# Opening and end of an attention reordered: key rows of 256 bytes, the second half of the keys turned in step 1, first weights converted seven steps sooner

## The chip and the metric

The kernel runs on one core of a Trainium2 chip. The metric is the device time of one execution in microseconds, lower is better; the times shown are medians over repeated executions. The core has five engines with a queue of instructions each: TensorE (PE in the profile, PEld for its weight loads) for matmuls and transposes, VectorE (DVE), ScalarE (ACT), GpSimd (POOL), and SyncE (SP), which here issues nearly all DMAs. Each engine works through its own queue in the order in which the program was written, so an instruction that waits holds everything behind it on that engine. The profile is one execution recorded by the hardware profiler; its times count from the start of the span.

## The reference

Attention with a bias that depends on positions, and behind it two small feed-forward blocks. B = 2, H = 8 heads, S = 576 tokens, D = 64; all inputs are float32, and the two weight groups of the feed-forward blocks come as float64.

```python
scores = scale * q @ k.T                                   # (B, H, S, S)
x = log1p(|i - j|) / log1p(max(i, 1))                      # (S, S), one number per pair
bias = relu(x * w1 + b1) @ w2                              # hidden 32 -> 8 heads
attn = softmax(scores + bias)                              # sum + 1e-9 below
x = concat_heads(attn @ v)                                 # (1152, 512)
y = ((x @ w_a) * (x @ w_b)) @ w_out                        # 512 -> 1536 -> 512
h = y @ w_in                                               # 512 -> 1024
solu = h * softmax(h);  ln = (solu - mean) / sqrt(var + 1e-6) * g_ln
out = ln @ w_out2                                          # 1024 -> 512
```

## The kernel before

Products in float32 precision are made from pairs of rounded parts: a value is split into a high part (float32r) and a low part, the difference, and TensorE multiplies the parts.

**The order.** Nothing is scheduled by a planner: the program writes each engine's order out by hand. After a preamble come nine turns T = 0 to 8 of an opening, then a loop over steps n = 0 to 76. Step n works on several stages of the pipeline at once. There are nine units (a block of 128 query rows of one batch; the last unit, number 8, has 64 rows of each batch), each of eight steps, one per head: 72 steps, and the loop runs on for five drain steps. A string, ORDER, gives the order of the parts in a step: b is the biased scores and their minimum of step n-1 on VectorE (L401), h the reciprocal of the sums and the scaling of step n-2 on POOL (shares, L413 to L415), p the exponential of step n-1 on ScalarE (L408), t the transposes of step n-3 (L423, L432) with copies out, s the scores of step n on TensorE (L388), v the values of a pair of heads (L452), o and u the bias, k and l the two halves of queries and keys turned in the step before, i and j the output of a finished unit, and x whatever was put down for the step by `later`.

**Bias.** A table (tabs) of x * w1 for all distances is made by matmuls with one row (`table`); the part for small row numbers comes first, the low part later. For each of 36 groups of 16 rows (T), `bias_hidden` makes four tiles h by Relu (L351 on VectorE, L353 on ScalarE, chosen by HIDDEN), `bias_sums` multiplies them by w2bd, a block matrix made by POOL from w2 (L213), and `bias_out` scales the sums by rp (made by `scales`, L221) into st on ScalarE (L371) and sends st by DMA into the bias tile of 128 rows. Groups 0 to 7 are made in the opening; a unit's first biased scores need all eight. SECOND_T gives the steps for groups 8 to 15.

**Keys and queries.** `fetch` loads a chunk of 128 tokens of four heads (a group g is four heads; ks[b, g] is four chunks and a short one of batch b). `twice` makes the high and the low part of a chunk (L268, L269; for queries a copy on POOL, L271), `turn` transposes it on TensorE (L281), and `keep_high` copies it into kst, the transposed keys (ScalarE, L298), or into qhi (L305); `keep_low` makes qlo on VectorE (L318). Group ks[0, 0] and the first queries (first_in) are turned in the opening; ks[0, 1] with the second queries (second) behind it; ks[1, 0] and ks[1, 1] in the steps that KEYS gives, with `twice` one step before. One DMA brings a whole group except its short chunk: each partition takes four neighbouring rows of a head, 1024 bytes, so that chunk c holds every fourth token, and its copy into kst writes with a stride of four:

```python
cols = slice(c, NC * P, NC) if c < NC else slice(NC * P, S)
nc.scalar.copy(kst[:, u, g * HG:(g + 1) * HG, cols], ps)
```

**First weights.** The words of the first four pieces of w_a and w_b (float64, two chunks c of 128 columns) are loaded and turned into float32 during the last unit by `first_one`, a generator of six stages: the load; Abs on ScalarE (L97) and a clamp on VectorE (L98); one word operation on VectorE (L103); two more (L105, L106); the high part on ScalarE (L566); the low part on VectorE (L568). FIRST gives the steps of the stages, counted from step 64. EARLY gives the steps, counted from 64 too, in which three blocks `gated(c, tg)` of 24 matmuls are put between the last parts of the attention; `product` follows each one step later. The space for these words is that of the h and st tiles, after step 56. All other pieces (the third chunk first) are loaded after the last values of the attention, into space which these free, and converted by `convert` while TensorE runs the other gated blocks. Tiles of scores, bias sums, tables and gated blocks share two PSUM buffers in turn (ps_s); those of transposes share three (ps_t).

Of the kernel before, what the change touches and what calls it, by code (L numbers as in the profile page):

```python
# [17 lines left out]
P = 128  # L18
# [7 lines left out]
ORDER = ("kbhvioljptsxu", "kbihlospjtvxu")  # L26
TURN = 55

KEYS = (4, 5, 5, 6, 7, 7, 8, 9, 11, 11)
SECOND_T = (1, 3, 6, 8, 10, 12, 13, 14)  # L30
LAST_T = (48, 50, 52, 54)

HIDDEN = (("vava", "vvva", "vvva", "vvvv", "vvva", "vvvv", "vvva", "vava"), ("vvvv", "avvv"))

FIRST = ((0, 1, 2, 3, 6, 7), (0, 3, 4, 5, 6, 7), (1, 6, 7, 8, 10, 11), (4, 7, 8, 8, 11, 11))
# [5 lines left out]
EARLY = {(0, 0): 8, (0, 1): 10, (1, 0): 11}  # L41
# [12 lines left out]
def tile_kernel(ctx, tc, q, k, v, w1, b1, w2, w_a, w_b, w_out, w_in2, w_out2, g_ln, psi, rpsi, out):  # L54
# [101 lines left out]
    with ExitStack() as actx:  # L156
# [27 lines left out]
        nc.scalar.dma_start(psi_i, psi[:, UW:].rearrange("(o c) t -> o c t", o=1))  # L184
        nc.scalar.dma_start(b1r, b1.rearrange("(o m) -> o m", o=1))
        nc.scalar.activation(warm, ident[:, 0:1], AF.Exp)
# [4 lines left out]
        nc.scalar.dma_start(rp_in, rpsi)  # L191

# [22 lines left out]
        def scales():  # L215

            ps = ps_t.tile([P, 4, NG // 16], F32, tag="t", name="ps_rp")
            for c in range(4):
                for qd in range(4):
                    nc.tensor.matmul(ps[32 * qd:32 * qd + 32, c], order4[:, c].rearrange("p g h -> p (g h)"), rp_in[:, qd::4], start=True, stop=True)  # L220
            nc.vector.tensor_copy(rp.rearrange("p (c k) -> p c k", c=4), ps)  # L221

        kst = ac.tile([P, B, H, S], F32R, name="kst")
# [8 lines left out]
        def fetch(w):  # L232
# [3 lines left out]
            if src == "k" and c < NC:  # L236

                if c == 0:
                    nc.sync.dma_start(raws[at, g], k[at, heads, 0:NC * P, :].rearrange("h (p r) d -> p h (r d)", r=NC))
                fetched[w] = raws[at, g][:, :, c * D:(c + 1) * D]  # L240
                return
# [17 lines left out]
        def twice(w, engine=nc.gpsimd):  # L259

            nat = fetched[w]
            if w[0] == "k":
                if w[3] < NC:
                    x, nat = nat, room(w)
                    fetched[w] = nat
                else:
                    x = nat[:, :, 1, :]
                nc.vector.tensor_copy(nat[:, :, 0, :].bitcast(F32R), x)  # L268
                engine.tensor_tensor(out=nat[:, :, 1, :], in0=x, in1=nat[:, :, 0, :], op=ALU.subtract)  # L269
                return  # L270
            nc.gpsimd.tensor_scalar(nat[:, :, 1, :], nat[:, :, 0, :], 1.0, 1.0, op0=ALU.mult, op1=ALU.mult)  # L271
# [20 lines left out]
        def keep_high(w):  # L292
# [3 lines left out]
            if src == "k":  # L296
                cols = slice(c, NC * P, NC) if c < NC else slice(NC * P, S)
# [184 lines left out]
        for b in range(B):  # L482
            for g in range(2):
                i = b * 2 + g
                raws[b, g] = arena[0][:, i * nr:(i + 1) * nr].rearrange("p (h x) -> p h x", h=HG)
# [4 lines left out]
        for w in first_in + second:  # L490
            fetch(w)
        nc.sync.dma_start(psi_l, psi[3:4, low + 3 - 12:half + 3])
        N0 = P // 16
        for j in range(2):
            nc.gpsimd.memset(vtl[(1 - j) * TL:(2 - j) * TL, :, :, j, :], 0.0)
        made = [[w] for w in first_in] + [second[0:3], second[3:5], second[5:]]
        for T in range(N0 + 1):
            if T < N0:
                bias_hidden(T)
            for w in made[T]:  # L500
                twice(w, nc.vector if w in first_in else nc.gpsimd)
            if T == 1:
                scales()
            if T > 0:
# [4 lines left out]
                if T <= len(first_in):  # L509
                    keep(first_in[T - 1])  # L510
            if T == 6:
                for dst, ps in table(low, half - low, psi_l, low - 12):
                    nc.scalar.copy(dst, ps)
# [4 lines left out]
        for w in second:  # L518
            turn(w)
            keep(w)  # L520
# [17 lines left out]
        for T in range(N0, S // 16):  # L538
# [8 lines left out]
            out_at.setdefault(n + 1, []).append(T)  # L547
        steps = [(u, h) for u in range(len(units)) for h in range(H)]
# [43 lines left out]
        for n in range(len(steps) + 5):  # L592
            for part in ORDER[n >= TURN]:
# [363 lines left out]
```

## Time and the profile before

| | |
|---|---|
| median of 3 runs | 553.75 us (553.64 to 553.91) |
| the profiled execution | 554.66 us |
| its span, first to last instruction | 552.8 us |
| TensorE busy | 534.8 us, 97% |
| VectorE busy | 421.4 us, 76% |
| ScalarE busy | 291.4 us, 53% |
| GpSimd busy | 173.9 us, 31% |

The attention takes the first 223 us or so, the feed-forward blocks the rest. Shares are means over stages with different limits; "busy" of TensorE counts the modelled length of pipelined matmuls. A row of a timeline gives the start and length in us, engine, line, operation, the tile written and the tiles read, how many such instructions follow one another, and, in brackets, the idle time of the engine before them with what ended it. Listed lengths on one engine can overlap by about 0.1 us. SPq and ACTq are DMA issues from the queues of SyncE and ScalarE.

### The profile page before, as it was taken

The numbers are of one execution on the slowest core, as the hardware profiler recorded it, in microseconds if no ns is written. First come the engines' busy times: TensorE is split into PE (matmuls) and PEld (weight loads), VectorE is DVE, ScalarE is ACT, GpSimd is POOL, SyncE is SP. The second block draws the span as 40 slices with busy tenths as digits, with TensorE's granted clock in tenths as the row PEclk, the third lists the DMA queues.
The fourth block names the chain that finished last, engine by engine and source line by source line (L and its number), as shares of the span: only waits on it lengthen the run. The fifth ranks groups of instructions, "written<-read, shape, count | busy, mean of one in ns | idle before, by whom it ended". The sixth has DMA issues, their size and how long they took to land.

```text
span 552.8 us, 12368 instructions
## 1 busy us (share of the span) xinstructions
PE 534.8 (97%) x4868; PEld 473.1 (86%) x4868; DVE 421.4 (76%) x895; ACT 291.4 (53%) x592; POOL 173.9 (31%) x277
## 2 busy tenths in 40 slices
PE   6978999999999998999999999999999999999997
PEld 2556788888888888999999999999999988888887
DVE  3858899999997687497799898889885566666661
ACT  4878877878787663445555334532443433222221
POOL 3237554545446642122222122233222530000000
PEclk9999999999999998999999999999999999999999
DMA  4494543332347110543445343444310000000001
GB/s 116 121 235 87 118 107 75 77 71 70 83 119 198 34 42 1 160 147 120 151 147 154 116 151 116 127 136 157 114 39 2 0 1 20 20 19 20 19 20 57
DMA packets 47581, 49.32 MB, mean 89 GB/s; under 512 B 23198, under 2 KB 37795, under 8 KB 47524
## 3 DMA queue, kind: packets, MB, share of 16 engines
q1 hardware_dynamic: 47238, 48.52, 31.3%
q8 instruction: 38, 0.62, 0.5%
q14 instruction: 19, 0.16, 0.1%
q10 hardware_dynamic: 286, 0.03, 0.1%
HBM read 34.37 MB, written 2.36 MB: 66 GB/s over the span
## 4 chain that ended last, share of the span: by engine, by line
PE 74%; DVE 10%; issue 3%; ACT 2%; POOL 2%; DMA 0%; DVEq 0%; ACTq 0%; POOLq 0%
PE pm L124 27%; PE po L124 11%; PE py L854 9%; PE ph L794 9%; PE px L452 4%; PE pt L423 4%; PE s L388 4%; PE bps L361 3%; DVE e L401 3%; POOL e L415 2%; DVE h L351 2%; PE pl L835 1%; DVE et L428 1%; PE tp_q L281 1%; ACT kst L298 1%
## 5 line engine op out<-in xcount | busy, mean ns | idle before, releaser
L98 POOL TENSOR_SCALAR f<-f 128x512 f32<-128x512 f32 x48 | 41.3, 862 | 140.2 <-ACT f L97 130.4
L415 POOL TENSOR_SCALAR e<-e,rec 128x576 f32<-128x576 f32 x72 | 60.2, 837 | 70.1 <-DVE rec L414 68.1
L124 PE MATMUL pm<-xhi,abh 128*128 128x384 f32 x240 | 80.2, 334 | 0.0
L124 PE MATMUL pm<-xhi,abl 128*128 128x384 f32 x240 | 80.2, 334 | 0.0
L124 PE MATMUL pm<-xlo,abh 128*128 128x384 f32 x240 | 80.2, 334 | 0.0
L408 ACT ACTIVATE e<-e,nm 128x576 f32<-128x576 f32 x72 | 55.8, 775 | 27.9 <-DVE nm L401 21.3
L351 DVE TENSOR_SCALAR h<-tabs 128x576 f32<-128x576 f32 x122 | 67.0, 590 | 0.0
L401 DVE CUSTOM_DVE_ANT_0 e<-s,bias 128x576 f32<-128x576 f32 x72 | 54.0, 749 | 7.6 <-PE s L388 5.8
L423 PE MATMUL pt<-ident,e 128*128 128x128 f32 x288 | 45.5, 281 | 5.6 <-POOL e L415 4.0
L143 ACT COPY one<-pm 128x384 f32<-128x384 f32 x36 | 17.3, 480 | 61.4 <-PE pm L124 61.4
L124 PE MATMUL po<-gh,oh 128*128 128x384 f32 x144 | 48.5, 337 | 0.6 <-DVE x2s L725 0.6
L124 PE MATMUL po<-gl,oh 128*128 128x384 f32 x144 | 48.4, 336 | 0.0
L124 PE MATMUL po<-gh,ol 128*128 128x384 f32 x144 | 48.4, 336 | 0.0
L361 PE MATMUL bps<-h,w2bd 128*32 128x288 f32 x576 | 47.2, 427 | 1.0 <-DVE nm L401 0.6
L124 PEld LDWEIGHTS pm<-xlo,abh 128*128 128x128 f32 x240 | 45.0, 188 | 0.0
L124 PEld LDWEIGHTS pm<-xhi,abh 128*128 128x128 f32 x240 | 45.0, 188 | 0.0
L124 PEld LDWEIGHTS pm<-xhi,abl 128*128 128x128 f32 x240 | 45.0, 188 | 0.0
L423 PEld LDWEIGHTS pt<-ident,e 128*128 128x128 f32 x288 | 32.2, 140 | 14.2 <-POOL e L415 8.4
L106 DVE SCALAR_TENSOR_TENSOR f<-words,f 128x512 int32<-128x512 int32 x48 | 42.2, 879 | 1.6
L388 PE MATMUL s<-kst,qhi 128*128 128x288 f32 x160 | 40.4, 334 | 0.3 <-ACT st L371 0.2
L452 PE MATMUL px<-et,vsb 128*32 128x128 f32 (+1 forms) x1280 | 40.3, 263 | 0.1
L452 PEld LDWEIGHTS px<-et,vsb 128*32 128x32 f32 x1280 | 34.1, 110 | 7.1 <-issue 1.9
(136 smaller groups left out, 1246.3 us busy)
## 6 DMA issues: line engine op xcount, KB each, us to landing
bias<-st SPq DMA_DIRECT2D x40, 288.0 KB, 3.5
words<-in_moe_w_out_dram SPq DMA_DIRECT2D x20, 512.0 KB, 3.7
words<-in_moe_w_a_dram SPq DMA_DIRECT2D x12, 512.0 KB, 3.4
words<-in_moe_w_b_dram SPq DMA_DIRECT2D x12, 512.0 KB, 3.6
words<-in_moe_w_in_dram SPq DMA_DIRECT2D x8, 512.0 KB, 3.7
nat_q<-in_q_dram SPq DMA_DIRECT2D x16, 128.0 KB, 3.4
arena_hi<-in_k_dram SPq DMA_DIRECT2D x4, 512.0 KB, 4.5
vsb<-in_v_dram SPq DMA_DIRECT2D x16, 128.0 KB, 3.8
```

The lines of the kernel that those rows point to most:

```text
L106: nc.vector.scalar_tensor_tensor(out=b, in0=words[:, :, 0], scalar=29, in1=b, op0=ALU.logical_shift_right, op1=ALU.bitwise_or)
L124: nc.tensor.matmul(ps, w, x, start=(i == 0), stop=(i == n - 1))
L351: nc.vector.tensor_scalar(h, win, sc, 0.0, op0=ALU.add, op1=ALU.max)
L361: nc.tensor.matmul(bps[32 * qd:32 * qd + 32, a, 0:SH], w2bd, h[:, a * SH:(a + 1) * SH], start=True, stop=True)
L388: nc.tensor.matmul(ps[:, a, 0:SH], w, kst[:, b, h, a * SH:(a + 1) * SH], start=(m == 0), stop=(m == len(mm) - 1))
L401: nc.vector.tensor_tensor_reduce(out=halves(e), in0=ps[:, :, 0:SH], in1=halves(bias_t[it][:, h, :]), op0=ALU.add, op1=ALU.min, scale=1.0, ...
L408: nc.scalar.activation(e, e, AF.Exp, bias=nm, scale=-1.0, accum_out=sums[:, h:h + 1])
L415: nc.gpsimd.tensor_scalar(e, e, rec[:, h:h + 1], 1.0, op0=ALU.mult, op1=ALU.mult)
L423: nc.tensor.transpose(pt[:, c, :], e[:, j * TL + c * P:j * TL + (c + 1) * P], ident)
L452: nc.tensor.matmul(px[rows, p, cols], lhsT, rhs, start=(c == 0 and m == 0), stop=(c == NC), skip_group_check=True)
L794: nc.tensor.matmul(ph[u][:, a], x[:, kc, cols], w[:, kc, a * 512:(a + 1) * 512], start=(i == 0), stop=(i == 3 * KD - 1))
L854: nc.tensor.matmul(ps, x[:, c, :], w[:, c, cols], start=(i == 0), stop=(i == 3 * KF - 1))
```

## The change

- The four chunks of a key group come by four DMAs with rows of 256 bytes, and a chunk holds 128 neighbouring tokens, so its copy into kst is dense.
- The DMAs of b1 and psi_i move from ScalarE's queue to SP's; on ScalarE's queue w2 and rp_in come ahead of the load of the exp table. rp is made before the opening's turns and copied by ScalarE.
- In the opening keep_low of the first queries comes one turn later; the vtl memsets move to turn 2; the low table moves from turn 6 to turn 8, copied by VectorE; the second group is fetched in pieces in turns 0 to 4; HIDDEN gives two more Relu of the first eight groups to ScalarE.
- The second group's keys are converted by VectorE alone, just ahead of step 0, and turned and kept in part x of step 1. The sums of group 8 move from step 1 to step 0.
- The keys of batch 1 are converted by POOL alone (before: the cast on VectorE, the subtraction on POOL), and KEYS moves most of them by a step.
- FIRST moves the conversion of the first weights from steps 64 to 75 to steps 57 to 69; EARLY moves two of the three gated blocks one step forward; from step 72 on part x comes ahead of t and v.

```diff
-ORDER = ("kbhvioljptsxu", "kbihlospjtvxu")
-TURN = 55
-KEYS = (4, 5, 5, 6, 7, 7, 8, 9, 11, 11)
-SECOND_T = (1, 3, 6, 8, 10, 12, 13, 14)
+ORDER = ("kbhvioljptsxu", "kbihlospjtvxu", "kbihlospjxtvu")
+TURN, DRAIN = 55, 72
+KEYS = (5, 6, 6, 7, 7, 8, 9, 10, 11, 11)
+SECOND_T = (0, 3, 6, 8, 10, 12, 13, 14)
-HIDDEN = (("vava", "vvva", "vvva", "vvvv", "vvva", "vvvv", "vvva", "vava"), ("vvvv", "avvv"))
-FIRST = ((0, 1, 2, 3, 6, 7), (0, 3, 4, 5, 6, 7), (1, 6, 7, 8, 10, 11), (4, 7, 8, 8, 11, 11))
+HIDDEN = (("vvva", "vvva", "vvva", "vvva", "vvva", "vvva", "vava", "vava"), ("vvvv", "avvv"))
+FIRST = ((-7, -6, -5, -4, 1, 2), (-7, -5, -4, -3, 2, 3), (-6, -3, -2, -1, 3, 4), (-2, 0, 1, 2, 4, 5))
-EARLY = {(0, 0): 8, (0, 1): 10, (1, 0): 11}
+EARLY = {(0, 0): 8, (0, 1): 9, (1, 0): 10}
@@ preamble
-        nc.scalar.dma_start(psi_i, psi[:, UW:].rearrange("(o c) t -> o c t", o=1))
-        nc.scalar.dma_start(b1r, b1.rearrange("(o m) -> o m", o=1))
-        nc.scalar.activation(warm, ident[:, 0:1], AF.Exp)
+        nc.sync.dma_start(b1r, b1.rearrange("(o m) -> o m", o=1))
+        nc.sync.dma_start(psi_i, psi[:, UW:].rearrange("(o c) t -> o c t", o=1))
         nc.scalar.dma_start(w2r, w2.rearrange("(o m) h -> o m h", o=1).to_broadcast([4, HID, H]))
         nc.scalar.dma_start(rp_in, rpsi)
+        nc.scalar.activation(warm, ident[:, 0:1], AF.Exp)
@@ scales
-            nc.vector.tensor_copy(rp.rearrange("p (c k) -> p c k", c=4), ps)
+            nc.scalar.copy(rp.rearrange("p (c k) -> p c k", c=4), ps)
+        scales()
@@ fetch
-                if c == 0:
-                    nc.sync.dma_start(raws[at, g], k[at, heads, 0:NC * P, :].rearrange("h (p r) d -> p h (r d)", r=NC))
-                fetched[w] = raws[at, g][:, :, c * D:(c + 1) * D]
+                fetched[w] = raws[at, g][:, c]
+                nc.sync.dma_start(fetched[w], k[at, heads, c * P:(c + 1) * P, :].rearrange("h p d -> p h d"))
@@ twice
-        def twice(w, engine=nc.gpsimd):
+        def twice(w, engine=nc.gpsimd, rounds=nc.gpsimd):
-                nc.vector.tensor_copy(nat[:, :, 0, :].bitcast(F32R), x)
+                rounds.tensor_scalar(nat[:, :, 0, :].bitcast(F32R), x, 1.0, 1.0, op0=ALU.mult, op1=ALU.mult)
@@ keep_high
-                cols = slice(c, NC * P, NC) if c < NC else slice(NC * P, S)
+                cols = slice(c * P, min(S, (c + 1) * P))
@@ the opening
-        for w in first_in + second:
+        for w in first_in:
             fetch(w)
-        for j in range(2):
-            nc.gpsimd.memset(vtl[(1 - j) * TL:(2 - j) * TL, :, :, j, :], 0.0)
-        made = [[w] for w in first_in] + [second[0:3], second[3:5], second[5:]]
+        made = [[w] for w in first_in] + [second[0:1], [], []]
         for T in range(N0 + 1):
             if T < N0:
                 bias_hidden(T)
             for w in made[T]:
-                twice(w, nc.vector if w in first_in else nc.gpsimd)
-            if T == 1:
-                scales()
+                twice(w, nc.vector if w in first_in else nc.gpsimd, nc.vector)
+            if T > 1 and T - 2 < len(first_in):
+                keep_low(first_in[T - 2])
             if T > 0:
                 bias_sums(T - 1)
                 if T <= len(first_in):
                     turn(first_in[T - 1])
                 bias_out(T - 1)
                 if T <= len(first_in):
-                    keep(first_in[T - 1])
-            if T == 6:
+                    keep_high(first_in[T - 1])
+            if T == 2:
+                for j in range(2):
+                    nc.gpsimd.memset(vtl[(1 - j) * TL:(2 - j) * TL, :, :, j, :], 0.0)
+            if T == N0:
                 for dst, ps in table(low, half - low, psi_l, low - 12):
-                    nc.scalar.copy(dst, ps)
+                    nc.vector.tensor_copy(dst, ps)
+            for w in second[T + (T > 0):T + 2 if T < 5 else T + 1]:
+                fetch(w)
...
-        for w in second:
-            turn(w)
-            keep(w)
+        def turn_second():
+            for w in second:
+                turn(w)
+                keep(w)
+
+        later(1, turn_second)
...
+        for w in second[1:]:
+            twice(w, nc.vector, nc.vector)
         steps = [(u, h) for u in range(len(units)) for h in range(H)]
...
-            for part in ORDER[n >= TURN]:
+            for part in ORDER[(n >= TURN) + (n >= DRAIN)]:
```

## Rows read from the trace of the kernel before

**Rows 1.** Table of stretches: stretch, its length, busy us of each engine, clock.

```profile
core 0: us, PE busy (x) PEld busy (x) DVE busy (x) ACT busy (x) POOL busy (x), PEclk, DMA share, GB/s
32.00:48.00 16.00, 11.75 (x125) 8.06 (x124) 11.46 (x30) 10.93 (x22) 8.82 (x15) 1.00 0.86 196
174.00:186.00 12.00, 11.93 (x185) 10.24 (x187) 8.31 (x25) 9.13 (x23) 9.18 (x20) 1.00 0.52 152
206.40:213.00 6.60, 4.06 (x17) 4.05 (x17) 6.53 (x16) 2.93 (x7) 3.12 (x4) 0.74 0.01 2
```

**Rows 2.** Timeline of the opening, 0 to 26 us.

```profile
2.39 0.59 ACTq L190 DMA_DIRECT2D raw<-in_w_dram  x1
...
6.95 1.85 POOL L213 TENSOR_SCALAR w2bd<-raw 32x8 f32<-32x8 f32 x4 [5.26 <-DMA raw<-in_w_dram]
...
8.85 2.17 PE L361 MATMUL bps<-h,w2bd 128*32 128x288 f32 x16 [0.46 <-POOL w2bd L213]
...
12.74 0.69 DVE L318 SCALAR_TENSOR_TENSOR qlo<-tp_q,qhi 128x512 fp32r<-128x512 f32 x1 [3.43 <-ACT qhi L305]
...
15.04 1.20 PE L361 MATMUL bps<-h,w2bd 128*32 128x288 f32 x16
...
17.01 0.28 DVE L268 CAST arena_lo<-arena_hi 128x256 fp32r<-128x256 f32 x1
...
17.68 1.37 DVE L351 TENSOR_SCALAR h<-tabs 128x576 f32<-128x576 f32 x3
...
22.96 0.96 PE L201 MATMUL table<-psi_l,psi_r 1*32 1x224 f32 x16
```

**Rows 3.** Groups of ScalarE instructions, 0 to 32 us: count, busy us, mean ns.

```profile
L298 ACT CAST kst<-tp_k 128x512 fp32r<-128x512 f32 x8 | 8.5, 1136 | 0.1
L371 ACT ACTIVATE st<-bps,rp 128x576 f32<-128x576 f32 x8 | 5.9, 741 | 4.5 <-PE bps L361 3.7 <-ACT st L371 0.7
L353 ACT ACTIVATE h<-tabs 128x576 f32<-128x576 f32 x8 | 5.8, 768 | 0.8 <-DVE tabs L210 0.8
```

**Rows 4.** Timelines of TensorE, ScalarE and VectorE, 27 to 40 us.

```profile
27.06 0.66 PE L281 MATMUL tp_q<-ident,nat_q 128*128 128x128 f32 x4
...
27.86 0.59 ACT L305 ACTIVATE qhi<-tp_q 128x512 fp32r<-128x512 f32 x1
...
32.00 0.76 DVE L401 CUSTOM_DVE_ANT_0 e<-s,bias 128x576 f32<-128x576 f32 x1 [1.11 <-DMA vsb<-in_v_dram]
...
39.22 0.29 DVE L268 CAST arena_hi<-arena_hi 128x256 fp32r<-128x256 f32 x1 [3.03 <-DMA arena_hi<-in_k_dram]
```

**Rows 5.** DMA issues over the span: count, KB each, median us to landing.

```profile
bias<-st SPq DMA_DIRECT2D x40, 288.0 KB, 3.5
...
words<-in_moe_w_a_dram SPq DMA_DIRECT2D x12, 512.0 KB, 3.4
...
nat_q<-in_q_dram SPq DMA_DIRECT2D x16, 128.0 KB, 3.4
```

**Rows 6.** Timelines of VectorE and TensorE, 205 to 209 us.

```profile
206.00 0.43 DVE L98 TENSOR_SCALAR single<-single 128x512 f32<-128x512 f32 x1 [1.94 <-ACT single L97]
...
208.95 0.69 PE L423 MATMUL pt<-ident,e 128*128 128x128 f32 x4 [2.54 <-POOL e L415]
```

**Rows 7.** Groups of POOL instructions, whole span: count, busy us, mean ns.

```profile
L271 POOL TENSOR_SCALAR nat_q<-nat_q 128x256 f32<-128x256 f32 x18 | 8.4, 471 | 0.1
...
L269 POOL TENSOR_TENSOR arena_hi<-arena_hi 128x256 f32<-128x256 f32 x4 | 3.3, 834 | 2.8 <-DVE arena_hi L268 2.8
```

**Rows 8.** Timelines of VectorE and TensorE, 237 to 241 us.

```profile
237.89 0.68 DVE L111 TENSOR_TENSOR abl<-f,abh 128x512 fp32r<-128x512 f32 x1
...
240.12 0.33 PE L124 MATMUL pm<-xhi,abh 128*128 128x384 f32 x1
```

**Rows 9.** Busy time of the conversions' tile (single) alone, 190 to 221 us: VectorE, ScalarE.

```profile
190.00:221.00 31.00, 12.59 (x20) 4.91 (x8) 0.94 0.06 19
```

**Rows 10.** Timelines of SP's queue and ScalarE, 175 to 178 us.

```profile
175.12 0.38 SPq L93 DMA_DIRECT2D words<-in_moe_w_a_dram  x1
...
177.10 0.60 ACT L305 ACTIVATE qhi<-tp_q 128x512 fp32r<-128x512 f32 x1
```

More of the change, by code (lines that the diff above doesn't have):

```diff
@@ L484, in tile_kernel @@
                 i = b * 2 + g
-                raws[b, g] = arena[0][:, i * nr:(i + 1) * nr].rearrange("p (h x) -> p h x", h=HG)
+                raws[b, g] = arena[0][:, i * nr:(i + 1) * nr].rearrange("p (c h d) -> p c h d", c=NC, h=HG)
         nats += pieced(arena[0][:, 4 * nr:]) + pieced(arena[1]) + pieced(arena[0][:, 0:2 * nr])
```

## Prediction

> **What bounds the kernel now.** I read the busy shares first: TensorE is busy for nearly the whole span (the table above), so time can only come from stretches where it waits or runs slowly. The table of stretches [rows 1] shows two. From 32 to 48 us TensorE is busy for 11.75 of 16 us, so 4.25 us are idle. From 206.4 to 213 it is busy for 4.06 of 6.6 us, at a mean granted clock of 0.74: 2.5 us are idle, and (1 - 0.74) x 6.6 = 1.7 us are lost to its lower level, 1.2 GHz. The edits act at both ends of the attention; between them TensorE carries a lead or a delay on.
>
> The timelines tell what makes the holes. The first bias sums wait for w2bd: POOL begins it at 6.95, when w2 has landed, and needs 1.85 us; the sums start at 8.85 [rows 2]. Sixteen of these matmuls take 2.17 us there and 1.20 us at 15.04: TensorE works at about half speed until some 15 us. VectorE meanwhile stands for 3.43 us, until 12.74, waiting for qhi, because the low half of the first queries is made at once [rows 2]. ScalarE's strided copies into kst take 1.14 us [rows 3], against 0.59 for the dense qhi, of the same size [rows 4]. When qhi starts, at 27.86, the last st is through; its transfer into the bias takes 3.5 us [rows 5], and the first biased scores start at 32.00, after a wait for a DMA [rows 4]. Under that transfer TensorE turns the second half, from 27.06 on, six tiles of about 0.66 us [rows 4]. By 39.22 VectorE has stood 3.03 us for key rows of the next batch [rows 4].
>
> At the end the clamp waits 1.94 us for ScalarE's Abs and starts at 206.00, with the biased scores of step 70 behind it; TensorE has nothing for 2.54 us, until 208.95 [rows 6], and is slow after that [rows 1].
>
> **Opening, up to the first biased scores.** The load of w2 becomes the first of its queue, at 0.72 instead of 2.39 [rows 2]. With the landing time unchanged POOL ends w2bd 1.67 us sooner, at 7.13, and the sums start at about 7.15. The load of psi_i goes behind three others on SP, to some 1.7; with the landing time of a block of queries, 3.4 us [rows 5], which is 60 times as large, it would be there at 5.1, about when the table's matmuls end. I take nothing; each us beyond would be a us of opening. Queries and keys leave 0.6 us later; the first key chunk is wanted at about 9.0.
>
> A key group was one DMA of 512 KB; it becomes four of 128 KB, issued about 0.5 us apart, at some 3.4 us to landing each [rows 5]. VectorE takes one per 2 us, so this is hidden. The dense copy saves 1.14 - 0.59 = 0.55 us on each of 16 copies, four of them here.
>
> With keep_low one turn later VectorE runs straight on, and ScalarE limits. After the first qhi becomes possible, at about 10.3, it has six copies (3.3), eight Relu (8 x 0.77) and seven st (7 x 0.74) [rows 3, 4]: 14.6 us as listed. Listed durations overlap by about 0.1 us, so 12.6, and I add 1.6 for waits on half-speed matmuls: the last st ends at 24.5, 3.4 us sooner.
>
> What is late next is VectorE's own queue. The low table now comes after the last sums: TensorE takes 0.96 us for it [rows 2], done at 24.8. Then VectorE has two copies (0.7), the four Relu of T=8 (three take 1.37 at 17.68, so 1.8) and five key conversions, 0.67 us each as from 17.01 to 17.68 [rows 2]: 3.3. The first biased scores start at 30.6, with the bias landed at 28.1. Of 3.4 us of lead 1.4 is left.
>
> **Steps 1 to 12.** The turning of the second half loses its cover. ScalarE has exp of step 0 and six copies in a row, to 35.2; a Relu and the next exp stand behind. On POOL share 0 ends at 35.8, TensorE follows with transposes, scores, sums and transposes, and the biased scores of step 3 start at 37.0, where the kernel before had them just behind the cast of 39.22 [rows 4]. VectorE does not stand for keys then: their issues follow ten loads of v, at 31.4, so the first chunk lands at 34.8, wanted at 39: 4 us of cover. The casts of the second batch move to POOL, at 0.47 us each on the row of the query copy; with the subtraction at 0.83 a chunk costs 1.3 us there [rows 7]. Steps 5 and 6, with two chunks each, take some 3.6 us of POOL, against 3 of TensorE, so part of the 2.4 us is at risk; elsewhere TensorE limits, and carried on by hand step 9 comes about 3.5 us ahead. TensorE idles 4.25 us between 32 and 48 [rows 1], so the lead can hardly pass 4.0. The other bound is 2.0 us lost: six turned tiles uncovered (4.0) against a lead of 1.4, with little of the later hole won.
>
> One thing takes part of it back: between the sums of T=8, which end at 27.6, and step 1, at 31.2, TensorE has nothing. The idle 2.54 us at 206.4 were followed by 1.7 us lost to the clock [rows 1, 6]. I count that here at four in five, 1.4 us, and take the opening at -3.5 + 1.4 = -2.1 us (range -4.0 to +2.0). The Trainium skill, page "TensorE: Matmul & The Clock Gate", section "What's actually happening", says that the throttled state is the default and that activity releases it; the trace agrees at 206.4, and by that rule the wait costs the 1.7 for certain and the term is -1.8, while with the clock kept up it is -3.5.
>
> **The end of the attention.** All four pieces are ready by step 69, so gated(0,0) needs only the buffer of the scores of step 70, free at about 203.7. It can follow the values at 206.4 without a gap: 2.5 + 1.7 = 4.2 us go.
>
> Two prices. First, three gated blocks instead of two stand before the last values. These end where they did, at 223.4, but one block fewer, 4.17 us, follows until TensorE wants the third chunk, whose words are loaded into space that the last values free. VectorE ends its conversion with the piece of 237.89, TensorE starts on the chunk at 240.12 and needs that piece 2.1 us later [rows 8]: 3.6 us of slack against 4.17. ScalarE gets to the words about 1.2 us sooner, having no product in front, but block (1,2) now waits for its buffer: VectorE is through with it 9.1 us after the last values, and TensorE wants it at 8.35. I take +0.8; without the 1.2 us it is +2, without any wait 0.
>
> Second, steps 58 to 63 get three of the four conversions without their last subtraction. All twenty instructions take 12.59 us [rows 9], so these twelve some 7.5 us, where VectorE idled 3.7 of 12 us [rows 1]. And ScalarE's Abs waits for words: their load cannot leave before 175.12, as it waits for the last bias transfer [rows 10], and takes 3.4 us [rows 5], to 178.5; ScalarE is there at 177.10 [rows 10]. Behind Abs stand qhi and the exp of step 58, and POOL's share and the transposes wait for those. Unit 8 gives some back, since VectorE loses old conversions there. I take +1.0; 0 if all is absorbed, +4 if each delay reaches TensorE. The end is -4.2 + 0.8 + 1.0 = -2.4 (range -4.2 to +1.8).
>
> **Sum.** -2.1 - 2.4 = -4.5 us. The profiled execution took 554.66 us, 552.8 of them the span; it becomes 550.2. The median shown is 0.91 lower, 553.75, so I forecast 549.3.
>
> **Rivals.** (A) The end gains, the opening doesn't: the turning in step 1 and POOL's chunks eat what sums and keys gave. For it speaks that a lead of 3.4 shrinks to 1.4 in VectorE's queue; against it the wait of 3.03 us that goes. 553.75 - 2.4 = 551.4.
> (B) The opening gains, the end doesn't: the third chunk comes at the old time, and the 4.2 us only move behind the last values. For it speaks that the slack of 3.6 is less than a block; against it that ScalarE comes to the words sooner. 553.75 - 2.1 + 0.3 = 551.9.
> (C) Slower: the turning out of its cover. VectorE's queue of table, Relu and conversions holds the first biased scores past 32, and 4.0 us of turning come on top, at the low clock (+1.7), with the end at -2.4: +3.3 at full price, 557.0. It decides the sign once the first biased scores start after some 33 us. Against it: the rows put them at 30.6, 2.4 us short of that.
> (D) No change worth measuring: a level opening, and at the end +4 from the words and +0.8 from the buffer against -4.2: 554.4.
>
> **Chances.** The forecast, 547 to 551: 0.58; better 0.05; A 0.13; B 0.08; D 0.06; C 0.10. Within 0.2% (1.1 us, about what a measurement here can tell from no change) lie most of D and the edges of A and B: 0.10; slower by more 0.12, C and the edge of D; faster 0.78. The range runs from 546.4, both terms near their best (-3.7 each), to 553.0, past A and B.
>
> **What would show it.** Right: first bias sums near 7.2; last st near 24.5; first biased scores near 30.6, with VectorE never idle from the low table's copies on; no wait for key rows at step 4; the biased scores of step 3 before 38; no idle over 0.5 us and no lowered clock between 200 and 225; a wait under 1 us before the third chunk. Wrong: first biased scores after 32, TensorE held for POOL's chunks in steps 5 to 8, unit 7 longer by over 2 us with ScalarE waiting for words, or a hole of 2 to 4 us before the third chunk.

## The result, and the profile after

The change makes the kernel slower: 560.40 us median (559.86 to 561.19) against 553.69 (553.45 to 553.91) for the kernel before on the same chip, ratio 1.0122, 95% interval 1.0105 to 1.0140. The profiled execution has a span of 558.1 us, 5.3 more than before. Forecast were 549.3 us and a range up to 553.0: the sign was wrong.

The opening, up to the first biased scores, came out at its marks. From the timeline of after, 0 to 32 us:

```profile
3.15 0.96 POOL L213 TENSOR_SCALAR w2bd<-raw 32x8 f32<-32x8 f32 x4 [1.47 <-DMA raw<-in_w_dram]
...
7.09 2.91 PE L360 MATMUL bps<-h,w2bd 128*32 128x288 f32 x16 [0.94 <-DVE h L350]
...
23.82 0.74 ACT L370 ACTIVATE st<-bps,rp 128x576 f32<-128x576 f32 x1 [0.62 <-PE bps L360]
...
24.74 0.69 DVE L513 COPY tabs<-table 128x224 f32<-128x224 f32 x2 [4.69 <-PE table L201]
...
30.57 0.76 DVE L400 CUSTOM_DVE_ANT_0 e<-s,bias 128x576 f32<-128x576 f32 x1
```

The first sums at 7.09, the last st through at 24.56 and the first biased scores at 30.57 answer to 8.85 in [rows 2] and 32.00 in [rows 4]: a lead of 1.4 us. The sums waited for VectorE's Relu, though, and not for w2bd, which was through at 4.11. The end did not come out. Three timelines of after, VectorE and ScalarE from 174 to 184 us, then TensorE from 175 to 215:

```profile
179.15 0.43 DVE L98 TENSOR_SCALAR single<-single 128x512 f32<-128x512 f32 x1 [2.32 <-ACT single L97]
179.49 0.75 DVE L400 CUSTOM_DVE_ANT_0 e<-s,bias 128x576 f32<-128x576 f32 x1
...
178.42 0.69 ACT L97 ACTIVATE single<-words 128x512 f32<-128x512 f32 x1 [1.91 <-DMA words<-in_moe_w_a_dram]
179.01 0.59 ACT L304 ACTIVATE qhi<-tp_q 128x512 fp32r<-128x512 f32 x1
180.34 0.78 ACT L407 ACTIVATE e<-e,nm 128x576 f32<-128x576 f32 x1 [0.74 <-DVE rec L413]
...
180.39 0.50 PE L387 MATMUL s<-kst,qhi 128*128 128x288 f32 x2 [1.31 <-DVE rec L413]
...
183.45 0.53 PE L387 MATMUL s<-kst,qhi 128*128 128x288 f32 x2 [1.40 <-DVE nm L400]
```

ScalarE waits 1.91 us for the words, VectorE 2.32 us for ScalarE; the biased scores of step 58 (179.49) stand behind, and TensorE runs dry for 1.31 and 1.40 us. A table of stretches, columns as in [rows 1]: the stretch from the biased scores of step 58 to those of step 64, then the tile `single` alone in the same stretch (columns of VectorE and ScalarE only), then the drain:

```profile
179.49:197.70 18.21, 14.13 (x155) 11.35 (x159) 16.46 (x38) 10.01 (x25) 9.78 (x18) 0.91 0.21 60
...
179.49:197.70 18.21, 8.77 (x13) 2.07 (x3) 0.91 0.21 60
...
206.40:225.00 18.60, 18.60 (x335) 17.73 (x336) 8.54 (x22) 8.22 (x21) 5.83 (x11) 1.00 0.01 2
```

The same six steps of the kernel before:

```profile
177.21:189.54 12.33, 12.26 (x184) 10.62 (x184) 8.62 (x26) 8.91 (x22) 9.40 (x21) 1.00 0.34 112
```

They took 12.33 us with TensorE full, and take 18.21 us now with VectorE busy for 16.46, 8.77 of it conversion: 5.9 us more. The step before them, with the wait for the words, took 5.52 us for 2.77 (step 57 to 58: 173.97 to 179.49, and 174.44 to 177.21 before). The granted clock of 0.91 is not what made the six steps long: in end_alone, a run of the experiments below, it was 0.81, and they took the same 18.21 us:

```profile
180.82:199.03 18.21, 14.98 (x154) 12.42 (x158) 16.47 (x38) 9.97 (x25) 9.77 (x18) 0.81 0.20 57
```

The drain is what the prediction wanted: 206.4 to 225 without a gap at full clock, where [rows 1] had 2.5 us idle and a clock of 0.74. That didn't pay for the 8.6 us up to step 64.

For the experiments I read four marks in each trace: the starts of the biased scores of steps 57, 64 and 71, and of the first matmul on the third chunk (the first that reads `abh`). In all but one run 312.7 to 312.9 us follow the last mark (313.2 in later_no_ops), so everything is decided before it. The last column, from step 57 to the third chunk, is the end without the opening. Each row is one execution, and its time lies up to 1.5 us from the median of the run's executions.

| run | step 57 | step 64 | step 71 | third chunk | 57 to third chunk |
|---|---|---|---|---|---|
| before | 174.44 | 189.54 | 209.48 | 240.12 | 65.7 |
| after | 173.97 | 197.70 | 212.54 | 245.16 | 71.2 |
| open_alone | 173.82 | 188.92 | 208.86 | 239.51 | 65.7 |
| end_alone | 175.12 | 199.03 | 213.85 | 246.74 | 71.6 |
| abs_one_step | 173.36 | 195.32 | 210.14 | 242.20 | 68.8 |
| words_early | 173.96 | 197.85 | 212.67 | 246.08 | 72.1 |
| abs_later | 173.35 | 193.10 | 209.84 | 241.85 | 68.5 |
| no_word_ops | 174.21 | 195.83 | 209.92 | 242.74 | 68.5 |
| later_no_ops | 174.26 | 191.14 | 206.86 | 238.83 | 64.6 |
| spread | 174.63 | 192.74 | 213.07 | 243.30 | 68.7 |
| split_after | 175.31 | 196.69 | 212.55 | 245.04 | 69.7 |
| split_later | 174.59 | 193.59 | 210.16 | 242.50 | 67.9 |
| drain_order | 174.11 | 189.21 | 209.15 | 239.83 | 65.7 |
| split_drain | 175.40 | 190.52 | 208.76 | 242.53 | 67.1 |
| ready | 173.02 | 188.12 | 209.87 | 237.89 | 64.9 |
| ready_drain | 172.97 | 188.08 | 209.84 | 238.09 | 65.1 |
| casts_vector | 172.77 | 187.89 | 207.85 | 238.47 | 65.7 |
| split_casts | 174.24 | 189.35 | 207.61 | 236.82 | 62.6 |
| split_before | 172.05 | 187.16 | 205.40 | 234.61 | 62.6 |

### The profile page after: what moved, and what is told of

It reads as the page before. It is cut to its first block, busy times and chain, and to the rows that moved or that the text cites. A ratio compares the mean times of both kernels' runs of the same rounds, so it can differ in the third digit from the quotient of the medians.

```text
span 558.1 us, 12392 instructions
## 1 busy us (share of the span) xinstructions
PE 537.6 (96%) x4868; PEld 474.5 (85%) x4868; DVE 420.7 (75%) x889; ACT 284.9 (51%) x593; POOL 172.0 (31%) x282
## 4 chain that ended last, share of the span: by engine, by line
PE 81%; DVE 6%; POOL 4%; DMA 3%; issue 3%; ACT 1%; SPq 1%; POOLq 0%; DVEq 0%; ACTq 0%
PE pm L124 25%; PE po L124 13%; PE py L861 9%; PE ph L801 9%; PE bps L360 7%; PE px L451 5%; PE s L387 4%; PE pt L422 4%; POOL e L414 2%; DVE e L400 2%; PE pl L842 1%; PE tp_q L280 1%; DVE h L350 1%; DMA words<-in_moe_w_out_dram 1%; PE tp_k L280 1%
## 5 line engine op out<-in xcount | busy, mean ns | idle before, releaser
L414 POOL TENSOR_SCALAR e<-e,rec 128x576 f32<-128x576 f32 x72 | 59.0, 820 | 77.5 <-DVE rec L413 73.3
L97 ACT ACTIVATE f<-words 128x512 f32<-128x512 f32 x48 | 32.5, 677 | 18.0 <-DMA words<-in_moe_w_a_dram 7.7
```

Of the source, the lines that this page charges most:

```text
L414: nc.gpsimd.tensor_scalar(e, e, rec[:, h:h + 1], 1.0, op0=ALU.mult, op1=ALU.mult)
```

## Experiments

Runs of before scatter from 553.5 to 553.9 us on one chip (four runs) and from 551.7 to 556.7 on another (thirty), so each ratio is against runs of before on the same chip.

**Which half?** open_alone is after with the conversion stages, the early blocks and the orders of before; end_alone is before with those of after.

```
open_alone:  FIRST, EARLY, ORDER, TURN as before; no DRAIN
end_alone:   before.py + FIRST, EARLY, ORDER, DRAIN of after
```

> The opening, the keys and POOL's casts of the changed kernel, with FIRST, EARLY, ORDER and the drain of the kernel before. Theory W (the loss sits in the conversions that moved into unit 7): the biased scores of step 47 came 0.7 us earlier in the changed kernel, and the end is that of before, so 553.7 - 0.7 = 553.0 us (552.3 to 554.0). Rival O (the reordered opening loses, by the turning out of its cover and POOL's chunks, and the end only shows it): most of the 6.7 us remain, 558 to 560.

> The kernel before with FIRST, EARLY, ORDER and the drain of the changed kernel and nothing else. Theory W: the last values come 8 us later and one gated block fewer behind them gives 3 us back: about +5.5, 559 us (558 to 561). Rival O: the end gains what the prediction gave it, -2.4, so 551.3. Rival X (the two halves hurt only together, because the opening's order shifts DMAs against the words): near 553.7.

open_alone: 553.72 us, ratio 1.0002 (0.9985 to 1.0018). end_alone: 560.20 us, ratio 1.0122 (1.0095 to 1.0149). Both lie in the marks of theory W. The whole loss is the end's, and the opening is worth nothing that can be measured: the interval goes from 0.8 us faster to 1.0 slower.

**Wait or load?** Two suspects in steps 58 to 64: ScalarE's wait for words, and VectorE's conversions. abs_later moves the stages so that the words are there; no_word_ops keeps the stages and leaves out the three word operations of each early piece; later_no_ops does both.

```
abs_later:
-FIRST = ((-7, -6, -5, -4, 1, 2), (-7, -5, -4, -3, 2, 3), (-6, -3, -2, -1, 3, 4), (-2, 0, 1, 2, 4, 5))
+FIRST = ((-7, -4, -3, -2, 1, 2), (-7, -3, -2, -1, 2, 3), (-6, -1, 0, 1, 3, 4), (0, 2, 3, 4, 5, 6))
no_word_ops:
-            yield from single(words, f)
+            yield
+            yield
```

> The changed kernel; only FIRST differs: the loads stay at steps 57, 58 and 62, and Abs, clamp and word operations of each piece come two to three steps later, so that the words are there when ScalarE reaches Abs. Theory W1 (the wait for words is the loss: ScalarE stands 1.9 us at Abs, VectorE 2.3 us at the clamp, and the chain of scores behind it loses about as much again): most of the loss goes, 553 to 555. Theory W2 (the load on VectorE in unit 7 is the loss, the wait only a part): the wait's 2.8 us go, the rest stays, 557 to 558.5. Theory W3 (neither; order of the drain): no change, 560.

> The changed kernel without the three word operations (L103, L105, L106) of the first four pieces, so their low bits are missing; loads, Abs, clamp, high and low parts stay where they are. Its time tells what 12 operations of together some 8 us on VectorE cost. W2: all but the wait's 2.8 us of the loss goes, the last values 5 us earlier, 554.5 to 556. W1: little changes, 558.5 to 560, with the wait at step 58 as before.

> The kernel after with both suspected prices of the end taken away: the stages of the four early pieces as in abs_later (no engine waits for words), and without the three word operations of each piece, as in no_word_ops (some 7.4 us of VectorE's work is left out, and the weights of the first two pairs are then wrong). Theory W and L together (the loss in steps 58 to 70 is the wait plus VectorE's load, and nothing else): step 71 starts near 206 us, and the time is 550 to 553 us. If a third thing holds these steps, it stays at 555 us or more.

abs_later: 556.51 us, ratio 1.0066 (1.0044 to 1.0088). no_word_ops, one run, so without an interval: 557.42. later_no_ops: 553.97, ratio 1.0005 (0.9983 to 1.0027). By the last column either step alone takes 2.7 us off after, both together 6.6: two prices, of about equal size, and neither theory alone was right: the times of abs_later and no_word_ops lie between the marks. later_no_ops missed its upper mark by 1 us all the same. The word operations that it leaves out stand in before too, only later, so its 64.6 is no measure of the move alone. And they are not all of the second price: in no_word_ops steps 58 to 64 still take 16.0 us for 12.3, with VectorE's clamps waiting 1.36 and 1.97 us for ScalarE's Abs; that wait returns below.

abs_later moves the load as well as the Abs. Two runs were to move the wait alone:

```
words_early:   first stages (-8, ...), (-8, ...), (-7, ...), (-2, ...)
abs_one_step:  first piece (-7, -5, -5, -4, 1, 2)
```

> The kernel after with the words of the first three early pieces asked for one step sooner (steps -8, -8, -7), so that the first Abs finds them there, and nothing else changed: the load on VectorE and its steps stay. If ScalarE's wait for the words (1.91 us, and VectorE's of 2.32 us behind it) is a price of its own, it comes back: 557.5 to 558.5 us. If the load sets these steps anyway, and the wait only fills what VectorE would have spent later, 559.5 to 560.5 us.

> The kernel after with the first early piece's Abs and clamp one step later (step -5 in place of -6), all else the same. words_early left the wait standing: the words left no sooner, since their buffer comes free only when the last bias rows are written (174.6 us). Here the Abs comes after they have landed, so the wait of 1.9 us is gone, and VectorE's load in these steps is the same. If the wait is a price of its own: 557.5 to 559 us; if VectorE's load alone sets steps 58 to 64: 559.5 to 561 us.

words_early: 561.07 us, ratio 1.0135 (1.0109 to 1.0161). It removed nothing, and lies half a us above its marks. SP's queue, and then ScalarE, in words_early:

```profile
169.89 1.17 SPq L372 DMA_DIRECT2D bias<-st  x2
174.77 0.37 SPq L93 DMA_DIRECT2D words<-in_moe_w_a_dram  x1
...
178.59 0.68 ACT L97 ACTIVATE single<-words 128x512 f32<-128x512 f32 x1 [2.08 <-DMA words<-in_moe_w_a_dram]
```

The words leave at 174.77, as in after (174.70), because their buffer lies where the bias rows were: the chain that ended last, in after, shows what holds them.

```profile
169.90 0.53 SPq L372
170.43 0.05 issue
170.48 4.14 DMA bias<-st
174.62 0.02 issue
174.64 0.03 SPq L93
174.67 0.03 issue
174.70 3.58 DMA words<-in_moe_w_a_dram
```

So asking sooner does not help: with their buffer in this place the words land at about 178.3, and only the Abs can be moved. abs_one_step does that: 558.02 us, ratio 1.0089 (1.0064 to 1.0114), inside its mark for a price of its own. Its ScalarE:

```profile
178.21 0.67 ACT L97 ACTIVATE single<-words 128x512 f32<-128x512 f32 x1
179.21 0.69 ACT L97 ACTIVATE single<-words 128x512 f32<-128x512 f32 x1 [0.33 <-DMA words<-in_moe_w_b_dram]
```

The wait shrinks from 1.91 to 0.33 us and the end from 71.2 to 68.8, with every conversion still in the same steps but for the first clamp (0.43 us), which moved with its Abs.

**Are there steps with room?** spread puts the conversions mainly into the last unit, one or two operations to a step.

```
+FIRST = ((-7, -3, -2, -1, 1, 3), (-7, 0, 1, 2, 3, 4), (-6, 3, 4, 5, 6, 8), (0, 6, 6, 7, 8, 9))
```

> The kernel after with the words still loaded seven steps early, but their conversion spread over steps 61 to 73, in the steps of the last unit, which take 2.9 us each instead of 2.1, one or two VectorE operations to a step. Theory L (what is lost in abs_later is lost because VectorE's 12.6 us are put into short steps): 550.5 to 553 us, with step 64 within 1.5 us of open_alone's 188.9. If every conversion ahead of the drain costs what it takes wherever it stands, about 556 us.

557.37 us, ratio 1.0058 (1.0041 to 1.0076), with step 64 at 192.74: a miss for the theory that the last unit's steps have room, and 1.4 us above the other mark too. Two lines of its VectorE and one of its ScalarE show another price:

```profile
182.30 0.16 DVE L413 RECIPROCAL rec<-rec 128x1 f32<-128x1 f32 x1
184.44 0.43 DVE L98 TENSOR_SCALAR single<-single 128x512 f32<-128x512 f32 x1 [1.98 <-ACT single L97]
...
183.72 0.68 ACT L97 ACTIVATE single<-words 128x512 f32<-128x512 f32 x1
```

No DMA is late here: ScalarE did not stand before this Abs. VectorE is a step ahead of ScalarE, and the clamp stands in the same step as the Abs: VectorE waits until ScalarE has done the exp and the copy that stand before it, and the next biased scores wait with it. The 1.94 us of [rows 6] are a wait of the same kind.

**The clamp a stage later.** The split runs put VectorE's clamp into the next stage, in front of the first word operation.

```
 magnitude:
         nc.scalar.activation(f, words[:, :, 1].bitcast(F32), AF.Abs)
-        engine.tensor_scalar(f, f, WORD_MAX, WORD_MIN, op0=ALU.min, op1=ALU.max)
+        if engine is not nc.vector:
+            engine.tensor_scalar(f, f, WORD_MAX, WORD_MIN, op0=ALU.min, op1=ALU.max)
 first_one:
             magnitude(words, f, nc.vector)
             yield
+            nc.vector.tensor_scalar(f, f, WORD_MAX, WORD_MIN, op0=ALU.min, op1=ALU.max)
             yield from single(words, f)
split_after: on after; split_later: on abs_later; split_casts: on casts_vector (below); split_before: on before
```

> The kernel after with one change: VectorE's clamp of an early piece comes a stage later than ScalarE's Abs, together with the first word operation, so that VectorE doesn't wait in the same step for ScalarE to reach the Abs (the four such waits are 4.0 us in after). Theory P (this pairing holds the chain): 556 to 558 us. Theory W (only ScalarE's wait for the words and VectorE's load hold it): the waits move to the next minimum or exp, and it stays at 559.5 to 561 us.

> abs_later with the same change: no engine waits for words and VectorE waits for no Abs in its own step; what is left of the end's second price is VectorE's load of 12.6 us. Theory P: 2.3 us of waits go, 553 to 555 us. Otherwise 556 to 557 us.

> casts_vector (end of before, opening of after, rounding copies on VectorE) with the same change: the two waits of 1.95 us of VectorE for an Abs at 190.7 and 204.4, which stand in before too, go. Theory P: 549.5 to 552 us, faster than both kernels, and no idle of 2.5 us on TensorE at 207. Otherwise 553.5 us.

> The kernel before with the clamp one stage after the Abs and nothing else, to part the two gains of split_casts. If the gain of split_casts is in the clamp's place: 551 to 552.5 us; if it is in the opening: 553.5 us.

On after and abs_later it hardly helps: 559.68 us, ratio 1.0100 (1.0078 to 1.0121), and 557.47, ratio 1.0063 (1.0042 to 1.0084). Theory P missed in both; 559.68 lies in the mark of theory W, 557.47 half a us above the other mark. In split_after ScalarE still waits 2.06 us for the words, and VectorE's wait only moves to the queries' low half, whose high half stands behind that Abs. With the stages of before it is the best version: split_casts 551.01 us, ratio 0.9952 (0.9933 to 0.9970), split_before 550.39, ratio 0.9945 (0.9927 to 0.9963), both faster than before and after, split_before by 0.6 us more than its mark. The table of stretches of split_before, from step 64 to step 71 and on, and below it steps 64 to 71 of before:

```profile
187.16:205.40 18.24, 17.87 (x335) 16.15 (x335) 15.67 (x41) 12.39 (x30) 8.92 (x16) 1.00 0.10 32
205.40:212.00 6.60, 6.04 (x110) 5.67 (x109) 5.78 (x14) 2.97 (x7) 2.00 (x3) 1.00 0.00 0
...
189.54:209.48 19.94, 17.34 (x332) 15.67 (x332) 15.94 (x41) 12.83 (x30) 9.40 (x16) 1.00 0.10 29
```

Up to step 71 TensorE is idle for 0.37 us where it was 2.60, and these steps take 1.7 us less. Behind them the clock is 1.00, where the last row of [rows 1] had 0.74, and the stretch to the third chunk takes 1.4 us less. The hole went without one conversion moved to an earlier step, and without the new order.

**The order of the drain.** drain_order is after with the conversion stages of before; split_drain adds the clamp's stage and the casts on VectorE; ready and ready_drain, with the clamp's stage and the casts too, end the conversions by step 9, without and with the order (and the second block's step).

```
drain_order: FIRST as before, EARLY {(0, 0): 8, (0, 1): 9, (1, 0): 11}, DRAIN of after
ready, ready_drain:
+FIRST = ((0, 1, 2, 3, 5, 6), (0, 2, 3, 4, 5, 6), (1, 4, 5, 6, 7, 8), (4, 6, 7, 7, 8, 9))
```

> The kernel after with the conversion stages of before and only the order of the drain (gated blocks asked for ahead of the last turning and values, the second block a step sooner). If the new order by itself fills the 2.5 us in which TensorE stood before step 72, as the prediction had it, 549.5 to 551.5 us. If that idle time belongs to the late conversion, and the order only swaps equal work, 553 to 554.5 us, as open_alone.

> split_casts with the new order of the drain (conversion stages of before, gated blocks ahead of the last turning and values). drain_order showed no gain of that order while VectorE waits for the Abs at 205.7. If the order fills TensorE once that wait is gone, it is 0.5 to 2 us under split_casts; if it only swaps equal work, the same within 0.5 us.

> split_drain with the last stages of the early pieces sooner (all within the last unit, the last at its step 9), so that the third gated block doesn't wait 2.1 us for its weights as it did in split_drain (219.4 to 221.8). If the drain order pays once its weights are ready, it beats ready by 0.5 us or more, and split_casts too: 549 to 550.5 us. If the order only swaps equal work, and delays the last unit's values and with them what follows, 551 to 552.5 us or more.

> The same stages without the drain order (the order and the gated blocks' steps of before): the control for ready_drain. Load put a step or two earlier into the last unit's steps costs there what it is, and nothing waits for it at the end: 551 us, as split_casts, within 1 us.

drain_order: 555.93 us, ratio 1.0039 (1.0020 to 1.0058); split_drain: 555.75, ratio 1.0039 (1.0023 to 1.0055), against 0.9952 without the order: both slower than any of their marks. TensorE in drain_order:

```profile
206.92 0.41 PE L124 MATMUL pm<-xhi,first 128*128 128x384 f32 x1 [0.85 <-DVE rec L413]
...
221.26 0.62 PE L124 MATMUL pm<-xhi,first 128*128 128x384 f32 x2 [2.14 <-DVE first L575]
```

The order fills most of the hole at 207, and the third block then waits 2.14 us for weights converted too late. (The time of drain_order lies 1.4 us above its traced execution's 554.55, so its column, level with before, understates the loss.) With the weights ready the order is worth nothing: ready 552.87 us, ratio 0.9990 (0.9975 to 1.0005), ready_drain 553.13, ratio 0.9994 (0.9977 to 1.0011). ready missed its mark by 0.9 us; ready_drain is where the order only swaps equal work. TensorE in ready, then in ready_drain:

```profile
208.27 0.66 PE L423 MATMUL pt<-ident,e 128*128 128x128 f32 x4 [2.06 <-POOL e L415]
```

```profile
207.32 0.41 PE L125 MATMUL pm<-xhi,first 128*128 128x384 f32 x1 [1.15 <-DVE rec L414]
...
233.80 0.44 PE L125 MATMUL pm<-xhi,first 128*128 128x384 f32 x1 [0.83 <-DVE g L145]
```

It takes 0.91 us off the hole and gives 0.83 back, where the block after the values waits for its buffer. And ready lost 2.3 us of the end to split_casts (64.9 for 62.6) by having its conversions a step or two sooner: VectorE is busy for 19.18 of the 21.75 us from step 64 to 71, and the hole of 2.06 us is there again though the clamp has its new place.

**The opening's lost lead.** In after the chain that ended last runs on GpSimd from 40 to 56 us; some of its pieces:

```profile
47.15 0.75 POOL e L414
47.91 0.58 POOL arena_hi L267
...
48.56 0.74 POOL arena_hi L268
49.30 0.37 POOL nat_k L267
...
49.74 0.73 POOL nat_k L268
...
50.55 0.19 POOL rec L412
```

The share of one step waits behind two chunks of the next keys, each with a rounding copy (L267) that was VectorE's. casts_vector gives the copies back, on open_alone:

```
-        def twice(w, engine=nc.gpsimd, rounds=nc.gpsimd):
+        def twice(w, engine=nc.gpsimd, rounds=nc.vector):
```

> open_alone with the rounding copies of the second half of the keys back on VectorE (one word of the change undone). Theory G: the lead of 2 us at step 5 is lost in steps 6 to 11 because GpSimd, given these copies, subtracts and shares in one line and sets the pace; then steps 6 to 11 keep the lead, and the time is 551.5 to 552.5 us. Rival: ScalarE's copies out of PSUM or TensorE set the pace there, and GpSimd's chain is only the last to arrive: 553.5 us, as open_alone.

553.46 us, ratio 0.9982 (0.9963 to 1.0001): the rival's mark, not theory G's. In the trace the lead over open_alone is 1.0 us at step 11 (64.87 against 65.86) and still 1.05 at step 57. The clock fell near 34 us in open_alone and not in casts_vector, so the two are not quite alike. Over the traces in which it did not fall before step 11, steps 0 to 11 take 34.6 to 34.8 us with the copies on GpSimd (four runs), 33.6 with them on VectorE (three), and 33.3 with the opening of before (two): the copies cost about 1.1 us there, and 0.3 more is lost otherwise. But step 57 lies anywhere from 172.05 to 175.40 us over these executions, with either opening, and split_before, with the old one, has the earliest. What the opening is worth, 0.5 us or nothing, stays open.

## Why the prediction was wrong

**Opening up to the first biased scores (lead 1.4 us): right, the first sums by luck.** Sums, last st and first biased scores came within 0.1 us of their marks. Of the last two the mechanism holds as well: from the first qhi, at 11.08, to the last st ScalarE stood for some 0.7 us in all, and from the low table's copies to the biased scores VectorE did not stand. The sums were to start when w2bd ended, at 7.13, with w2's landing time unchanged; w2bd began at 3.15 and ended at 4.11, and the sums waited for a Relu. The lead itself differs from execution to execution: the first biased scores start at 31.4 to 32.0 us in the three traces with the old opening, at 30.0 to 31.25 in the sixteen with the new one.

**Steps 1 to 12 (a further gain of 2.1, less 1.4 for the clock): mis-sized.** The biased scores of step 3 came at 38.17, for 37.0, still ahead of 39.43 before, and no key rows were waited for. GpSimd's chunks were named as a risk to "part of the 2.4 us"; all of the lead over before was gone by step 10 (61.10 against 61.06). By the comparison of steps 0 to 11 above, the copies on GpSimd took about 1.1 us of it. The clock did fall in after:

```profile
31.00:37.00 6.00, 3.80 (x26) 2.99 (x24) 3.82 (x11) 5.37 (x12) 1.59 (x3) 0.84 0.91 205
37.00:43.00 6.00, 6.00 (x78) 4.47 (x78) 3.94 (x12) 3.03 (x8) 3.37 (x7) 0.87 0.73 146
```

That is (0.16 + 0.13) x 6 = 1.7 us lost to the lower level, for the 1.4 counted. The prediction drew on the Trainium skill, page "TensorE: Matmul & The Clock Gate", section "What's actually happening", by which the throttled state is the default and activity releases it, and read from it that the loss was certain. The trace of after agrees, with clocks of 0.84 and 0.87 behind waits of 0.88 and 1.79 us on TensorE; but of the sixteen traces with this opening only eight show the clock lowered between 31 and 37 us. abs_later and abs_one_step have waits of the same length (0.88 and 1.78 us) and a clock of 1.00, so the loss was not certain. Where the clock fell and the copies were on GpSimd, steps 0 to 11 took 35.3 to 35.7 us for 34.6 to 34.8, so it cost about 0.9 us. The term of -2.1 measured -0.5 in the trace of after and nothing in open_alone's time. This cost the forecast some 2 us.

**The end, "+1.0; 0 if all is absorbed, +4 if each delay reaches TensorE": the step that failed.** Up to step 64 the end takes 8.6 us more (2.75 in the step with the wait for the words, 5.9 in the six behind it), and 3.1 less from there to the third chunk. The 65.7 us from step 57 to the third chunk became 71.2, where -4.2 + 0.8 + 1.0 had made it 63.3. The parts were all in the prediction: 7.5 us of conversion for 3.7 us of VectorE's idle time, and ScalarE's words at 178.5 for 177.1. Two things were wrong. The idle time was taken from a stretch that begins at 174, and treated as if VectorE could use it at any moment; but an instruction ahead of the biased scores holds them, then the exp, the share and the transposes, and TensorE has only two buffers of scores to run ahead in (that the buffers are what ends its cover is argued, not tried). And the wait and the load add (abs_one_step and abs_later; no_word_ops; later_no_ops); the bound of 4 holds the load alone. With the wait as measured the bound should have been 7.5 - 3.7 + 2.3 = 6.1 in place of 4, and the sum at that bound is -2.1 - 4.2 + 0.8 + 6.1 = +0.6, no change. Even that credits all of the idle time; with none of it the sum is 7.5 + 2.3 = 9.8, and the 8.6 measured up to step 64 lie nearer to it.

**The gain of 4.2 us: not the order's to win.** The hole and the low clock did go in after. But ready and ready_drain show that the order trades a hole of 0.9 for a wait of 0.8, and split_before that the hole of before came from the clamp's place. (after with the old order was not run, so what the order is worth in after itself is not shown.) [rows 6] gave it: the wait before the clamp ended with ScalarE's Abs, and the words had long landed. I read which engine released the clamp and not what stood ahead of the Abs on that engine, in before:

```profile
204.22 1.14 ACT L566 CAST first<-single 128x512 fp32r<-128x512 f32 x2
205.26 0.71 ACT L97 ACTIVATE single<-words 128x512 f32<-128x512 f32 x1
```

The remedy was one operation a stage later, and is worth 3.1 us of the end.

**The price for the third chunk, +0.8: right in size.** The block after the values waits 0.48 us for its buffer in after, and 0.83 in ready_drain.

**The rivals.** Rival C had the sign, by a mechanism (the turning out of its cover) that didn't come. Rival D came nearest in its mechanism, a level opening and "+4 from the words", but was priced to no change. The observation that was to show the prediction wrong, the unit of steps 56 to 63 longer by over 2 us with ScalarE waiting for words, is the one that came.

## What to carry to other kernels

An operation slotted into a tight in-order loop can cost most of its duration, and its wait on top (here 8.77 us of conversions made six steps 5.9 us longer, and the wait for the words cost 2.4 us), unless the engine stands idle at that very place; a sum of idle time over a stretch is no cover. When one engine's operation feeds another's, put them a stage apart, so that the engine that runs ahead doesn't stop for the other's queue: on before that was worth 0.55%, while moving the work cost 1.2%; where VectorE's load or a late DMA set the pace (split_after, split_later) it was worth little. Before asking for a load sooner, look in the chain of waits for what frees its buffer.

## What was not expected of the hardware

A hole of two us on TensorE does not always lower the clock. The 2.54 us of [rows 6] were followed by 0.74; the same hole in ready (2.06 us, at 208.27) lies in a stretch, 205 to 215 us, at 1.00. The wait of 2.14 us for the third block's weights lies in a stretch at 1.00 in drain_order (215 to 225 us) and at 0.87 in split_drain (218 to 224). What tells these apart I haven't found; it is not the kernel. Of thirty executions of before on one chip eleven had a mean granted clock of 1.000 over the span, fifteen 0.997 and four 0.994, with medians of 552.5, 554.1 and 555.9 us, so by these means the 1.7 us that the prediction wanted back at the end are lost in some executions only. In split_before, where 0.37 us of the hole are left, all six had 1.000.

Key rows of 256 bytes cost nothing that shows here: up to 60 us of after, the chunks of 128 KB landed in a median of 2.6 us. The first four are issued over 1.6 us, so by an estimate from these two figures such a group is there 4.2 us after its first issue; the one DMA of 512 KB with rows of 1024 bytes took a median of 4.5 us in before.

The same code takes a us or two more or less in the middle of the attention, where nothing was changed: the three executions with the opening of before reached step 57 at 174.44, 175.12 and 172.05 us. An edit of the opening worth 0.5 us can't be judged by one trace of each.
